# First products as 11 block products of sums of blocks in place of 12, over groups of 1024 tokens

## The chip, the cores and the metric

The kernel runs on one core of a Trainium2 chip. The metric is the device time of one execution in microseconds (us). TensorE multiplies, VectorE (DVE) and ScalarE (ACT) read its results out of PSUM banks, GpSimd (POOL) works on SBUF alone, SyncE (SP) issues the DMAs.

## The reference

Three layers over 3072 tokens (4 batches of 768) and a model width of 384:

```python
# 1: decayed linear attention, per batch and head (8 heads of 48)
state = f[t, :, None] * state + outer(k[t], v[t]);  y[t] = q[t] @ state
# 2: a mixture of 8 experts, all tokens through all experts
P = exp(logits - max); 8 rounds of normalizing P over rows, then columns
out = sum over e of P[:, e] * (relu(x @ w1[e]) @ w2[e])      # 384 -> 1024 -> 384
# 3: a bilinear layer
((x @ w_a) * (x @ w_b)) @ w_out                               # 384 -> 1536 -> 384
```

w_a, w_b and w_out come as float64; the rest is float32.

## The kernel before

Every product of float32 accuracy is made of three passes over split operands: a high part H (a ScalarE copy to fp32r) and a low part L (the rest); the passes are H·H, H·L and L·H.

**The attention stage** runs 24 steps of 128 tokens. Each step ends with six DMAs that bring y to x's layout (L593), a ScalarE copy into xH and a VectorE subtraction into xL (L599, L600). Expert 0 is computed beside it, in 12 blocks of 256 tokens (function expert0), as entries that fill TensorE's time; its low parts are made on GpSimd (L637), its results go to DRAM (y0, L653). xH and xL hold all 3072 tokens in SBUF. The order of the instructions of a stage is written out by class Plan: a list schedule in which each entry has a cost, a priority and the buffers that it reads and writes; GAP = 0.2 us is charged from one engine's end to another's start, and LATE = 4 us for a load. The engines then run that fixed order, each its own, and wait on semaphores.

**The main stage** (L734 on) has units of weights: 14 of 512 hidden columns (experts 1 to 7) and 6 of 256 (the last layer). For each unit it goes over 6 blocks of 512 tokens. front() makes the first products: for each tile of 128 hidden columns nine products of 512 tokens (gemm_f, L276: 3 k tiles x 3 passes) in one PSUM bank pF, then H on ScalarE and L on VectorE out of the bank. back() makes the second products (gemm_t, L288: 384 columns wide, bank pR) and VectorE adds them to acc, all of whose 24 token tiles are in SBUF. After the last expert unit x2_split transposes acc and splits it into xH and xL again. A unit's weights are loaded and split on ScalarE and GpSimd while the unit before is computed (add_piece, L247, L249); float64 weights go through seven VectorE operations (to_f32, L192 to L200), once, since each weight is loaded once. Instructions that the planner's loop emits in the main stage all carry L847.

Of the kernel before, what the change touches and what calls it, by code (L numbers as in the profile page):

```python
# [112 lines left out]
def kernel(  # L113
# [89 lines left out]
    def load_unit(parts, tag):  # L203
        """parts: dram access patterns, of [128, n, m] or in the order of ROWS; H and L of each."""
        views, pieces = [], []
        o = None
        for src in parts:
            if o is None or src is parts[-1]:
                tg = "i" if o is None else "o"
                o = 0  # L210
                wh = wpool.tile([128, WT[tg]], F32R, tag=f"{tag}{tg}h", name="wh")
                wl = wpool.tile([128, WT[tg]], F32R, tag=f"{tag}{tg}l", name="wl")
            n = src.shape[1 if len(src.shape) == 3 else 0]
            m = src.shape[-1] // (1 if src.dtype == F32 else 2)
            cut = m if src.dtype == F32 or m <= 256 else m // 2
            hv, lv = (t[:, o:o + n * m].rearrange("p (n m) -> p n m", n=n) for t in (wh, wl))
            for j in range(n):
                for c in range(0, m, cut):
                    pieces.append((src, hv, lv, cut, j, c))
            views.append((hv, lv))  # L220
            o += n * m
        return views, pieces

    def add_piece(plan, prio, key, src, hv, lv, cut, j, c):
        """The load of one part of a unit, its H, its L."""
        wide = src.dtype != F32
# [4 lines left out]

        def get():
            if len(src.shape) == 3:
                sj = src[:, j, 2 * c:2 * c + 2 * cut] if wide else src[:, j, c:c + cut]
                nc.sync.dma_start(out=raw, in_=sj if wide else sj.bitcast(I32))
                return
            for hd in range(2):
                nc.sync.dma_start(out=raw[64 * hd:64 * hd + 64], in_=src[j, hd, :, :, c:c + cut].bitcast(I32))

        plan.add(prio, "SP", .05 + cut * (.0013 if not wide else .0026), [], [f"raw{n}"], get, LATE)  # L240
        got, gk = f32(raw), f"raw{n}"
        if wide:
            for x, fn in enumerate(to_f32(raw, cut, *cvs)):
                plan.add(prio + 1 + x, "DVE", (.07 + cut / 960) * (1 if x % 2 or x == 4 else .65),
                         [gk], ["cv"], fn)
            got, gk = f32(cvs[0][:, :cut]), "cv"
        plan.add(prio + 9, "ACT", .1 + cut / 1200, [gk], [key], lambda: nc.scalar.activation(  # L247
            out=hj, in_=got, func=AF.Copy))
        plan.add(prio + 10, "POOL", .05 + cut * .0023, [gk, key], [key], lambda: nc.gpsimd.tensor_tensor(  # L249
            out=lj, in0=got, in1=f32(hj), op=ALU.subtract))  # L250
# [637 lines left out]
```

## Time and profile before

| | us |
|---|---|
| median of 3 runs (lowest, highest) | 2339.33 (2337.92, 2340.45) |
| span of the profiled execution | 2336.7 |
| TensorE products busy | 2285.6 (98%) |
| VectorE busy | 1132.5 (48%) |
| ScalarE busy | 645.1 (28%) |
| GpSimd busy | 254.8 (11%) |
| chain of waits: L276 into pF, L288 into pR | 42%, 36% |

The span runs from the first to the last instruction of one execution. Products are pipelined and overlap in the records, so what one costs is the distance between the starts of two. "Idle before" is the time in which an engine stood still ahead of an instruction, with what ended it. The granted clock is a share of 2.4 GHz.

### The profile page before, as it was taken

Reading aid. Unit: us, or ns where it says so; the run is one execution under the profiler, and the core shown is the slowest. Engines: PE = TensorE matmul, PEld = TensorE weight load, DVE = VectorE, ACT = ScalarE, POOL = GpSimd, SP = SyncE. Lnnn points to the kernel's source line nnn. Section 1 sums busy time; section 2 is a strip of 40 time slices with the busy share of each in tenths; the row PEclk is TensorE's granted clock in tenths of the full one; section 3 lists DMA queues with packets and bytes.
Section 4 is the critical chain, followed back from the end, with each engine's and each line's share of the span. In section 5 each row is a group of like instructions: output and inputs, shape, how many; then the busy total and the mean of one; then the engine's idle time right before and its main releaser. Section 6 shows DMA issues by size and latency. Waiting matters only on the chain.

```text
span 2336.7 us, 38096 instructions
## 1 busy us (share of the span) xinstructions
PE 2285.6 (98%) x15883; PEld 2072.8 (89%) x15883; DVE 1132.5 (48%) x2278; ACT 645.1 (28%) x1342; POOL 254.8 (11%) x291
## 2 busy tenths in 40 slices
PE   5999999999999999999999999999999999999999
PEld 4888888999999999999999999999999988888888
DVE  7888888443333333333333333333336564667643
ACT  3555555452121212112121111111212233222221
POOL 2221212230010101001010010100100010001000
PEclk8899999999999999999999999999999999999999
DMA  6444333140000000000000000000000010111001
GB/s 123 94 89 83 77 79 61 32 136 11 27 23 5 28 1 28 15 13 28 1 28 12 16 27 1 27 3 26 24 8 25 17 37 22 33 32 37 29 18 68
DMA packets 174316, 84.41 MB, mean 36 GB/s; under 512 B 133440, under 2 KB 163392, under 8 KB 174144
## 3 DMA queue, kind: packets, MB, share of 16 engines
q1 hardware_dynamic: 174144, 81.97, 14.1%
q8 instruction: 125, 2.05, 0.4%
q14 instruction: 47, 0.39, 0.1%
HBM read 67.78 MB, written 9.44 MB: 33 GB/s over the span
## 4 chain that ended last, share of the span: by engine, by line
PE 88%; DVE 7%; ACT 1%; SPq 1%; DMA 1%; issue 1%; POOL 0%; DVEq 0%; ACTq 0%; POOLq 0%
PE pF L276 42%; PE pR L288 36%; PE pM L288 3%; PE pM L276 3%; DVE fi L422 1%; DVE X L479 1%; DMA xf<-q 1%; PE pO L578 1%; SPq L593 1%; DVE X L528 1%; PE pA L454 1%; DMA raw<-in_moe_w_dram 1%; PE pA L442 0%; DVE fi L414 0%; DVE fi L416 0%
## 5 line engine op out<-in xcount | busy, mean ns | idle before, releaser
L276 PE MATMUL pF<-xH,wl 128*128 128x512 f32 x1440 | 562.7, 391 | 0.0
L276 PE MATMUL pF<-xL,wh 128*128 128x512 f32 x1440 | 562.3, 390 | 0.0
L276 PE MATMUL pF<-xH,wh 128*128 128x512 f32 x1440 | 561.7, 390 | 0.0
L288 PE MATMUL pR<-wh,gh 128*128 128x384 f32 x1632 | 547.7, 336 | 0.0
L288 PE MATMUL pR<-wh,gl 128*128 128x384 f32 x1632 | 546.9, 335 | 0.0
L288 PE MATMUL pR<-wl,gh 128*128 128x384 f32 x1632 | 546.0, 335 | 0.0
L847 ACT ACTIVATE gh<-pF 128x512 fp32r<-128x512 f32 x336 | 200.8, 598 | 978.7 <-PE pF L276 978.7
L847 DVE SCALAR_TENSOR_TENSOR gl<-pF,gh 128x512 fp32r<-128x512 f32 x336 | 232.1, 691 | 488.6 <-ACT gh L847 488.3
L847 DVE SCALAR_TENSOR_TENSOR acc<-pR,prob,acc 128x384 f32<-128x384 f32 x336 | 207.4, 618 | 410.7 <-PE pR L288 409.8
L276 PEld LDWEIGHTS pF<-xH,wl 128*128 128x128 f32 x1440 | 270.2, 188 | 56.7
L276 PEld LDWEIGHTS pF<-xL,wh 128*128 128x128 f32 x1440 | 270.2, 188 | 53.8
L276 PEld LDWEIGHTS pF<-xH,wh 128*128 128x128 f32 x1440 | 270.4, 188 | 53.2
L288 PEld LDWEIGHTS pR<-wh,gh 128*128 128x128 f32 x1632 | 306.4, 188 | 4.6
L288 PEld LDWEIGHTS pR<-wl,gh 128*128 128x128 f32 x1632 | 306.4, 188 | 4.7
L288 PEld LDWEIGHTS pR<-wh,gl 128*128 128x128 f32 x1632 | 306.2, 188 | 0.0
L249 POOL TENSOR_TENSOR wl<-raw,wh 128x384 fp32r<-128x384 f32 (+1 forms) x112 | 127.7, 1146 | 1152.0 <-ACT wh L247 1141.7
L637 POOL TENSOR_TENSOR hl<-hf,hh 128x256 fp32r<-128x256 f32 x96 | 80.0, 836 | 310.5 <-ACT hf L635 305.4
L847 DVE TENSOR_TENSOR a<-a,pF 128x512 f32<-128x512 f32 x72 | 49.5, 687 | 129.8 <-PE pF L276 126.6
L249 POOL TENSOR_TENSOR wl<-cva,wh 128x256 fp32r<-128x256 f32 (+1 forms) x60 | 42.1, 702 | 497.8 <-ACT wh L247 497.8
L276 PE MATMUL pM<-xH,wh 128*128 128x256 f32 x288 | 90.1, 313 | 0.1
L247 ACT ACTIVATE wh<-raw 128x384 fp32r<-128x384 f32 (+1 forms) x112 | 61.8, 565 | 98.6 <-DMA raw<-in_moe_w_dram 53.0
L276 PE MATMUL pM<-xL,wh 128*128 128x256 f32 x288 | 82.6, 287 | 0.7 <-DVE xL L600 0.7
(126 smaller groups left out, 2174.3 us busy)
## 6 DMA issues: line engine op xcount, KB each, us to landing
raw<-in_moe_w_dram SPq DMA_DIRECT2D x96, 128.0 KB, 2.6
raw<-in_moe_w_dram SPq DMA_DIRECT2D x64, 192.0 KB, 2.3
nat_f<-in_f_logit_dram SPq DMA_DIRECT2D x24, 192.0 KB, 3.3
nat_q<-in_q_dram SPq DMA_DIRECT2D x24, 192.0 KB, 3.4
nat_k<-in_k_dram SPq DMA_DIRECT2D x24, 192.0 KB, 3.7
vn<-in_v_dram SPq DMA_DIRECT2D x24, 192.0 KB, 2.7
Y<-in_v_dram SPq DMA_DIRECT2D x96, 48.0 KB, 2.8
xf<-q SPq DMA_DIRECT2D x144, 32.0 KB, 2.0
```

The lines of the kernel that those rows point to most:

```text
L247: plan.add(prio + 9, "ACT", .1 + cut / 1200, [gk], [key], lambda: nc.scalar.activation(out=hj, in_=got, func=AF.Copy))
L249: plan.add(prio + 10, "POOL", .05 + cut * .0023, [gk, key], [key], lambda: nc.gpsimd.tensor_tensor(out=lj, in0=got, in1=f32(hj), op=ALU.su ...
L276: nc.tensor.matmul(out=ps, lhsT=a[:, kk, fs], rhs=b[:, kk, ts], start=(i == 0), stop=(i == 3 * KD - 1),)
L288: nc.tensor.matmul(out=ps, lhsT=a[:, off:off + 128], rhs=b, start=(start and i == 0), stop=(stop and i == n - 1))
L422: op(DVE, .34, [], [f"fi0{z}", f"fi1{z}"], lambda a=a, c=c: nc.vector.tensor_tensor(out=fi[:, :, :, a], in0=fi[:, :, :, a], in1=fi[:, :, : ...
L454: nc.tensor.matmul(out=A1[o:o + 56, 0, g, :].rearrange("j (b e) -> j b e", e=8), lhsT=pct(k3)[r:r + D, g, 0:56], rhs=qv[r:r + D, g, :, 1, :])
L479: nc.vector.copy_predicated(X[r, hd].rearrange("j g (b two e) -> j g b two e", two=2, e=n)[:, :, :, 1, :], mbc(r, o, nb, n), A1[r, lv].rea ...
L528: op(DVE, .34, [f"q3{z}", f"g32{z}"], [f"Xq{z}"], lambda hd=hd, r=r: nc.vector.tensor_tensor(out=X[r, hd, :, 32:64], in0=pct(q3)[r, :, 32: ...
L578: nc.tensor.matmul(out=ps[64 * hd:64 * hd + D, p * 128 + 64 * c:p * 128 + 64 * c + 64], lhsT=Y[0:kk, hd, c, p, :], rhs=X[0:kk, hd, 2 * p + ...
L593: nc.sync.dma_start(out=xf[64 * hd:64 * hd + 64, kk, :], in_=yT[r:r + 16].rearrange("d (p t) -> d p t", p=NP))
L637: op(POOL, .64, [f"hh{ft}", kf], [f"hl{ft}"], lambda hh=hh, hl=hl, hf=hf: nc.gpsimd.tensor_tensor(out=hl, in0=hf, in1=f32(hh), op=ALU.subt ...
L847: fn()
```

## The change

Two halves of a pair of hidden tiles (256 columns) and two halves of 1024 tokens, over three k tiles, are a block product of 2 x 3 by 3 x 2 blocks: 12 block products in before. After, sums of blocks of the weights and of x are made first, and 11 block products of these, added up in an order of seven chains, give the same four results. One job is one pair of hidden tiles for 1024 tokens. In CHAINS a line names the bank, its products as (sum of weights, sum of x), and what the chain yields. A chain accumulates in one of three PSUM banks (A, B, C); b1, b2 and c1 are copied out by ScalarE to a buffer z while the bank goes on accumulating, and t1, t2 and t3 are added to a z by VectorE.

The main stage goes by six phases: expert phases of groups 0 and 1, last layer of group 0, experts of group 2, last layer of groups 1 and 2. x is stored to DRAM (xd) and the nine sums of a group are loaded, made and split at the start of its phase (for the first, in the attention stage on GpSimd). The weights are loaded and split anew for each group; each job's five sums of weight blocks and the low parts are made on GpSimd. The float64 weights are converted once, during the expert phases, and written to DRAM as float32. Expert 0 and the logits read x from two blocks of 256 tokens. acc holds the 8 token tiles of one group. back() works on four hidden tiles, in two parts, with the priority of the job three further on.

```diff
+X_SUMS = [(1,), (1, "add", 3), (3,), (2,), (0, "subtract", 3), (0, "add", 1), (4, "subtract", 1), (5,), (3, "add", 4)]
+W_RAW = [(0, 0), (2, 2), (1, 9)]
+W_SUMS = [(4, 10, 1), (5, 9, 4), (6, 0, 5), (7, 10, 9), (8, 3, 2)]
+CHAINS = [
+    ("B", [(4, 0)], "b1"),
+    ("A", [(1, 5), (3, 3)], "t1"),
+    ("B", [(5, 1)], "b2"),
+    ("C", [(9, 6), (2, 7)], "c1"),
+    ("B", [(6, 2)], "t2"),
+    ("C", [(7, 8), (8, 7)], "t3"),
+    ("B", [(2, 3), (0, 4)], "t0"),
+]
...
-    xH = big.tile([128, KD, NT], F32R, name="xH")
-    xL = big.tile([128, KD, NT], F32R, name="xL")
+    xsum = [[big.tile([128, TB], F32R, name=f"xs{x}{n}") for x in "hl"] for n in range(NX)]
+    xd = [spill.tile([KD, 128, NT], F32, name=f"x{n}d") for n in (1, 2)]
...
+    b_x = [[sba.tile([128, KD, EB], F32R, name=f"x{x}{n}") for x in "HL"] for n in range(2)]
...
+    def w1_prep(plan, prio, n):
...
+        for kk, slot in W_RAW:
+            plan.add(prio, SP, .38, [] if phases[ph][0] == "moe" else [f"wd{e}"], [f"sg{j}{kk}"], get, LATE)
+        sk = [f"sg{j}{kk}" for kk in range(KD)]
+        for o, a, b in W_SUMS:
+            plan.add(prio + 1, POOL, .4, sk, [f"sg{j}s"], partial(
+                nc.gpsimd.tensor_tensor, out=st[:, o], in0=st[:, a], in1=st[:, b], op=ALU.subtract))
+        for x in range(2):
+            s = slice(5 * x, 5 * x + 5)
+            key = f"w1{n % 3}{x}"
+            plan.add(prio + 2, ACT, .65, sk + [f"sg{j}s"], [key], partial(
+                nc.scalar.activation, out=wh[:, s], in_=st[:, s], func=AF.Copy))
+            plan.add(prio + 3, POOL, 1.6, sk + [f"sg{j}s", key], [key], partial(
+                nc.gpsimd.tensor_tensor, out=wl[:, s], in0=st[:, s], in1=f32(wh[:, s]), op=ALU.subtract))
...
+    def x_sum(plan, prio, i, src, tmp, eng):
...
+        if len(src) > 1:
+            (ka, a), (kb, b) = src
+            plan.add(prio, eng, ce, [ka, kb], [key], partial(
+                tt, out=t, in0=a, in1=b, op=getattr(ALU, X_SUMS[i][1])))
+        plan.add(prio, ACT, .6, [key], [f"xs{i}"], partial(nc.scalar.activation, out=xh, in_=t, func=AF.Copy))
+        plan.add(prio, eng, ce, [key], [f"xs{i}"], partial(tt, out=xl, in0=t, in1=f32(xh), op=ALU.subtract))
...
-    p_F = ring("pF", 4, [128, 512], psb)
-    p_R = ring("pR", 4, [128, 512], psb)
+    p_F = ring("pF", 5, [128, 512], psb)
+    p_R = ring("pR", 3, [128, 512], psb)
+    NH = 6
+    b_z = ring("z", 9, [128, TB], sbb)
+    acc = ring("acc", TPG, [128, DM], sbb)
...
+        for bank, prods, what in CHAINS:
...
+            def mm(prods=prods, ps=ps, new=new):
+                for slot, x in prods:
+                    xh, xl = xsum[x]
+                    for a, b in ((wh, xh), (wh, xl), (wl, xh)):
+                        nc.tensor.matmul(out=ps, lhsT=a[:, slot], rhs=b, start=(new and i == 0),
+                                         stop=(i == 3 * len(prods) - 1), skip_group_check=not new)
...
+            if what in ("b1", "b2", "c1"):
+                plan.add(prio, ACT, .6, [kp], [kz], partial(nc.scalar.activation, out=z, in_=ps, func=AF.Copy))
+                continue
+            ft, t = {"t0": (0, 0), "t1": (1, 0), "t2": (0, 1), "t3": (1, 1)}[what]
+            if what == "t0":
+                ky, y = kp, ps
+            else:
+                ky, y = got[{"t1": "b1", "t2": "c1", "t3": "b2"}[what]]
+                plan.add(prio, DVE, .7, [kp], [ky], partial(nc.vector.tensor_tensor, out=y, in0=ps, in1=y, op=ALU.add))
...
+    def back(n, hs, ws):
...
+        prio = 1000 * (n + 3)
...
+            for part in range(2):
+                hp = [hs[2 * part + i][j * 128 // TB] for i in range(2)]
+                wp = ws[2 * part:2 * part + 2]
+                plan.add(prio, PE, .173 * 6, [h[0] for h in hp] + [w[0] for w in wp], [kr], partial(
+                    gemm_t, ps, [h[1:] for h in hp], [w[1:] for w in wp], off, part == 0, part == 1))
...
+    def x2(prio, t, at, ka):
+        plan.add(prio, PE, .33, [ka], [kr], tr)
+        kz, z = take_z()
+        plan.add(prio, ACT, .45, [kr], [kz], partial(nc.scalar.activation, out=z[:, :DM], in_=ps[:, :DM], func=AF.Copy))
+        plan.add(prio, SP, .1, [kz], [f"xd1{t * 128 // TB}"], lambda: nc.sync.dma_start(
+            out=xd[1][:, :, t * 128:t * 128 + 128].rearrange("k p t -> p k t"),
+            in_=z[:, :DM].rearrange("p (k t) -> p k t", k=KD)), 3.0)
```

## Rows read from the trace of the kernel before

**Rows 1.** Page, part 1: busy us of each engine (share) x instructions.

```profile
PE 2285.6 (98%) x15883; PEld 2072.8 (89%) x15883; DVE 1132.5 (48%) x2278; ACT 645.1 (28%) x1342; POOL 254.8 (11%) x291
```

**Rows 2.** Chain that ended last: start us, us, what; mid main stage.

```profile
1119.74 8.20 PE pF L276 x36
...
1127.94 8.34 PE pR L288 x48
```

**Rows 3.** Groups by line and form: count, busy us, mean ns, idle before, releasers.

```profile
L276 PE MATMUL pF<-xH,wh 128*128 128x512 f32 x1440 | 561.7, 390 | 0.0
...
L288 PE MATMUL pR<-wh,gh 128*128 128x384 f32 x1632 | 547.7, 336 | 0.0
...
L847 DVE SCALAR_TENSOR_TENSOR gl<-pF,gh 128x512 fp32r<-128x512 f32 x336 | 232.1, 691 | 488.6 <-ACT gh L847 488.3
...
L847 DVE SCALAR_TENSOR_TENSOR acc<-pR,prob,acc 128x384 f32<-128x384 f32 x336 | 207.4, 618 | 410.7 <-PE pR L288 409.8 <-ACT acc L847 0.7
...
L249 POOL TENSOR_TENSOR wl<-raw,wh 128x384 fp32r<-128x384 f32 x64 | 65.8, 1030 | 151.9 <-ACT wh L247 141.6 <-DMA acc<-y 10.3
...
L249 POOL TENSOR_TENSOR wl<-raw,wh 128x512 fp32r<-128x512 f32 x48 | 61.9, 1300 | 1000.1 <-ACT wh L247 1000.1
...
L847 DVE TENSOR_TENSOR a<-a,pF 128x512 f32<-128x512 f32 x72 | 49.5, 687 | 129.8 <-PE pF L276 126.6 <-ACT wh L247 2.7
```

**Rows 4.** Busy us by window: PE, PEld, DVE, ACT, POOL, PEclk, DMA share, GB/s.

```profile
0.00:487.33 487.33, 439.77 (x6588) 401.99 (x6589) 378.64 (x870) 253.03 (x634) 106.10 (x136) 0.96 0.39 79
...
487.33:2336.70 1849.37, 1845.79 (x9297) 1670.81 (x9296) 753.88 (x1408) 392.05 (x708) 148.73 (x155) 1.00 0.08 25
```

**Rows 5.** Timeline of VectorE and GpSimd, float64 conversions: start us, us, instruction.

```profile
1900.26 0.28 DVE L199 TENSOR_SCALAR cvt<-raw 128x256 int32<-128x256 int32 x1
...
1900.58 0.43 DVE L200 SCALAR_TENSOR_TENSOR cva<-cvt,cva 128x256 f32<-128x256 int32 x1
...
1901.70 0.69 DVE L847 TENSOR_TENSOR gl<-a,gh 128x512 fp32r<-128x512 f32 x1 [0.69 <-ACT gh L847]
...
1902.04 0.94 POOL L249 TENSOR_TENSOR wl<-cva,wh 128x256 fp32r<-128x256 f32 x1 [5.45 <-ACT wh L247]
...
1902.30 0.83 DVE L192 TENSOR_SCALAR cvt<-raw 128x256 int32<-128x256 int32 x1
...
1924.39 0.60 POOL L249 TENSOR_TENSOR wl<-cva,wh 128x192 fp32r<-128x192 f32 x1 [4.47 <-ACT wh L247]
...
1924.43 0.69 DVE L847 TENSOR_TENSOR a<-a,pF 128x512 f32<-128x512 f32 x1 [0.52 <-PE pF L276]
```

**Rows 6.** Timeline, hand-overs TensorE to ScalarE, VectorE to TensorE.

```profile
1127.78 0.33 PE L288 MATMUL pR<-wh,gh 128*128 128x384 f32 x1
...
1127.98 0.60 ACT L847 ACTIVATE gh<-pF 128x512 fp32r<-128x512 f32 x1 [1.44 <-PE pF L276]
...
397.96 0.66 DVE L513 TENSOR_TENSOR k<-k,g 112x256 f32<-112x256 f32 x1
...
398.67 0.60 PE L518 MATMUL pO<-ident,k 112*128 112x112 f32 x4 [0.76 <-DVE k L513]
```

**Rows 7.** Timeline of ScalarE, attention stage.

```profile
390.92 0.38 ACT L632 ACTIVATE hh<-pM 128x256 fp32r<-128x256 f32 x1 [1.73 <-PE pM L276]
...
393.46 0.52 ACT L599 ACTIVATE xH<-xf 128x384 fp32r<-128x384 f32 x1
```

**Rows 8.** SP's queue: last stores of y0; line L238's issues (ns), its landing.

```profile
483.88 4.49 SPq L653 DMA_DIRECT2D y<-ys  x2
...
L238 SPq DMA_DIRECT2D raw<-in_moe_w_dram x96: 536/578/1812, 6.0 to 1675.1; - x96
...
DMA to landing us min/median/max: 2.3/2.6/5.3
```

**Rows 9.** Timeline of TensorE, then a window (as in rows 4).

```profile
403.98 1.15 PE L442 MATMUL pA<-bq,bk 48*64 48x64 f32 x32 [1.31 <-ACT bk L432]
...
406.00:407.00 1.00, 1.00 (x6) 0.80 (x4) 0.92 (x3) 0.68 (x2) 0.00 (x0) 0.50 0.00 0
```

More of the change, by code (lines that the diff above doesn't have):

```diff
@@ L201, in to_f32 @@
         ]
[L203 to L222, printed above, removed]
@@ L224, in add_piece, with take_raw @@
-    def add_piece(plan, prio, key, src, hv, lv, cut, j, c):
-        wide = src.dtype != F32
-        hj, lj = hv[:, j, c:c + cut], lv[:, j, c:c + cut]
+    def take_raw(m):
         n = count["raw"] % len(raws)
         count["raw"] += 1
-        raw = raws[n][:, :2 * cut if wide else cut]
-        def get():
[L233 to L250, printed above, removed]
@@ L270, in gemm_f, with add_piece @@
+    def add_piece(plan, prio, key, parts, hj, lj, reads=()):
+        m = hj.shape[-1]
+        rk, raw = take_raw(m)
+        def get():
+            for p0, n, src in parts:
+                nc.sync.dma_start(out=raw[p0:p0 + n], in_=src.bitcast(I32))
+        plan.add(prio, "SP", .05 + m * .0013, reads, [rk], get, LATE)
+        split_ops(plan, prio + 9, f32(raw), rk, hj, lj, key, m)
+    def gemm_f(ps, w, ft, x):
         wh, wl = w
+        xH, xL = x
         fs = slice(ft * 128, ft * 128 + 128)
-        ts = slice(t0, t0 + n)
@@ L646, in expert0 @@
                 fs = slice(part * n, part * n + n)
-                wk = [f"w{part // 2}o{x}" for x in range(KD, KD + FT)]
+                wk = [f"e0o{part // 2}{x}" for x in range(FT)]
                 op(PE, .98, hk + wk, [km], partial(
@@ L710 @@
     sinkhorn(plan, 1000 * NSTEP, 0, ROUNDS1, "T", p_T)
-    NUNIT = E * (DFF // FU)
-    NUNIT2 = DFF2 // FU2
-    units = [("moe", u) for u in range(NUNIT)] + [("out", u) for u in range(NUNIT2)]
-    views = {}
-    def load(plan, n, lo, hi, pieces):
-        for x in range(lo, hi):
-            key = f"w{n % 2}{'oi'[len(pieces) - x > n_out(n)]}{x}"
-            add_piece(plan, 1000 * NBLK * (n - 1) + 4000 * x / len(pieces) + 500, key, *pieces[x])
-    def n_out(n):
-        return FT if units[n][0] == "moe" else 2 * FT2
@@ L725 @@
-    NBLK = NT // 512
-    views[2], pieces2 = load_unit(moe_parts(2), "w0")
-    for x in range(KD):
-        add_piece(plan, 1000 * (NSTEP + 10) + x, f"w0i{x}", *pieces2[x])
+    phases = [("moe", 0), ("moe", 1), ("out", 0), ("moe", 2), ("out", 1), ("out", 2)]
+    jobs = []
+    for ph, (kind, g) in enumerate(phases):
+        for u in range((E - 1) * (DFF // FU) if kind == "moe" else DFF2 // FU):
+            for f in range(0, FT, 2):
+                if kind == "moe":
+                    jobs.append((ph, u, f, 1 + u // (DFF // FU), u % (DFF // FU) * FU + f * 128))
+                else:
+                    jobs.extend((ph, u, f, n, u * FU + f * 128) for n in range(2))
@@ new lines, with get @@
+    PW = 2 * 128
+    def w1_prep(plan, prio, n):
+        ph, _, _, e, c = jobs[n]
+        if phases[ph][0] == "moe":
+            parts = moe_rows(e, c, PW)
+        else:
+            parts = [[(0, 128, wd[e][kk * 128:kk * 128 + 128, c:c + PW])] for kk in range(KD)]
+        j = n % 2
+        st, (wh, wl) = stage[j], w1s[n % len(w1s)]
+        for kk, slot in W_RAW:
+            def get(kk=kk, slot=slot):
+                for p0, m, src in parts[kk]:
+                    nc.sync.dma_start(out=st[p0:p0 + m, slot:slot + 2, :].rearrange("p s f -> p (s f)"), in_=src)
+            plan.add(prio, SP, .38, [] if phases[ph][0] == "moe" else [f"wd{e}"], [f"sg{j}{kk}"], get, LATE)
[10 more added lines that the diff above has]
+                nc.gpsimd.tensor_tensor, out=wl[:, s], in0=st[:, s], in1=f32(wh[:, s]), op=ALU.subtract))
@@ L729 @@
+    prio = 1000 * 12
+    ab = [(f"xr{n}", b_xr[n]) for n in range(2)]
+    for blk, z, i in ((1, 0, 0), (3, 1, 2), (None, 0, 1), (0, 0, 4), (4, 0, 8), (1, 1, None), (4, 0, 6), (0, 0, 5),
+                      (2, 0, 3), (5, 1, 7)):
+        prio += 700
+        if blk is not None:
+            x_load(plan, prio - 400, 0, blk, *ab[z])
+        if i is not None:
+            x_sum(plan, prio, i, ab if len(X_OF[i]) > 1 else [], ab[z], POOL)
+    w1_prep(plan, 1000 * 12, 0)
     with tc.manual_schedule():
@@ new lines, with take_z, convert @@
+    xraw = {b: (f"xr{b}", sbb.tile([128, TB], F32, name=f"xr{b}")) for b in range(2 * KD)}
+    cva = ring("cva", 2, [128, 256], sbb, I32)
+    cvt = sbb.tile([128, 256], I32, name="cvt")
+    count["cv"] = 0
+    def take_z():
+        m = count["z"] % len(b_z)
+        count["z"] += 1
+        return f"z{m}", b_z[m]
+    def convert(prio, n, r0, c, m):
+        rk, raw = take_raw(2 * m)
+        x = count["cv"] % 2
+        count["cv"] += 1
+        src = (w_a, w_b, w_out)[n].bitcast(I32)[r0:r0 + 128, 2 * c:2 * c + 2 * m]
+        plan.add(prio, SP, .7, [], [rk], lambda: nc.sync.dma_start(out=raw, in_=src), LATE)
+        for i, fn in enumerate(to_f32(raw, m, cva[x], cvt)):
+            plan.add(prio + 1 + i, DVE, (.07 + m / 960) * (1 if i % 2 or i == 4 else .65),
+                     [rk], [f"cva{x}", "cvt"], fn)
+        plan.add(prio + 9, SP, .2, [f"cva{x}"], [f"wd{n}"], lambda: nc.sync.dma_start(
+            out=wd[n][r0:r0 + 128, c:c + m], in_=f32(cva[x][:, :m])), 3.0)
@@ new lines, in front @@
+    def front(n):
+        ph, u, f, ab, _ = jobs[n]
+        kind = phases[ph][0]
+        prio = 1000 * n
+        wh, wl = w1s[n % len(w1s)]
+        banks, got = {}, {}
+        hs = [[None, None], [None, None]]
+        if kind == "moe" or ab == 1:
+            for ft in range(2):
+                for t in range(2):
+                    m = count["h"] // 4 * 2 % NH + ft
+                    hs[ft][t] = (f"g{t}{m}", *b_h[t][m])
+            count["h"] += 4
+        for bank, prods, what in CHAINS:
+            prio += 10
+            new = bank not in banks
+            if new:
+                banks[bank] = take("F", p_F)
+            kp, ps = banks[bank]
+            def mm(prods=prods, ps=ps, new=new):
+                i = 0
+                for slot, x in prods:
[3 more added lines that the diff above has]
+                                         stop=(i == 3 * len(prods) - 1), skip_group_check=not new)
+                        i += 1
+            plan.add(prio, PE, .227 * 3 * len(prods), [f"xs{x}" for _, x in prods] +
+                     sorted({f"w1{n % 3}{s // 5}" for s, _ in prods}), [kp], mm)
+            if what in ("b1", "b2", "c1"):
+                kz, z = take_z()
+                got[what] = kz, z
+                plan.add(prio, ACT, .6, [kp], [kz], partial(nc.scalar.activation, out=z, in_=ps, func=AF.Copy))
[3 more added lines that the diff above has]
+                ky, y = kp, ps
+            else:
+                ky, y = got[{"t1": "b1", "t2": "c1", "t3": "b2"}[what]]
+                plan.add(prio, DVE, .7, [kp], [ky], partial(
+                    nc.vector.tensor_tensor, out=y, in0=ps, in1=y, op=ALU.add))
+            if kind == "out" and ab == 0:
+                if what == "t0":
+                    ky, y = take_z()
+                    plan.add(prio, ACT, .6, [kp], [ky], partial(
+                        nc.scalar.activation, out=y, in_=ps, func=AF.Copy))
+                a_of[what] = ky, y
+                continue
+            kh, hh, hl = hs[ft][t]
@@ L783, in front @@
                 nc.vector.tensor_tensor, out=hl, in0=a, in1=f32(hh), op=ALU.subtract))
         return hs
-    def back(n, b, hs):
-        kind, u = units[n]
-        later = n == len(units) - 1 and b == NBLK - 2
-        prio = 1000 * (NBLK * n + b + later) + 100
-        w = ftiles(views[n][-1])
-        hk = [f"g{x}{m}" for m, _, _ in hs for x in "hl"]
-        hp = [h[1:] for h in hs]
-        for j in range(TPB):
-            t = b * TPB + j
+    def back(n, hs, ws):
+        ph, u, _, e, _ = jobs[n]
+        kind, g = phases[ph]
+        last = n + 1 == len(jobs) or jobs[n + 1][0] != ph
+        prio = 1000 * (n + 3)
+        for j in range(TPG):
+            t = g * TPG + j
@@ L838 @@
[L838 to L844 removed]
+                nc.tensor.transpose(ps[:, kk * 128:kk * 128 + 128], at[:, kk * 128:kk * 128 + 128], ident)
+        plan.add(prio, PE, .33, [ka], [kr], tr)
+        kz, z = take_z()
```

224 lines of the change are left out of this document (119 added, 105 removed).

## The prediction

> **What bounds the kernel now.** I read the busy times first [rows 1]: TensorE's products are busy 2285.6 us of a span of 2336.7 us. Busy time counts overlapped products, so the chain of waits comes next [rows 2]. From the middle of the kernel to its end it is TensorE alone: 36 products of 512 columns in 8.20 us, then 48 of 384 columns in 8.34 us, each piece beginning where the one before ended (1119.74 + 8.20 = 1127.94). So one 512-column product costs 8.20/36 = 0.2278 us and one 384-column product 8.345/48 = 0.1738 us, far below their busy means of 390 and 336 ns [rows 3]. The windows [rows 4] cut the span at 487.33 us, the first product of the main stage: before it TensorE is busy 439.8 of 487.3 us; after it 1845.8 of 1849.4 us, at a granted clock of 1.00 (2.4 GHz). In the main stage VectorE is busy 753.9 us (41%), ScalarE 392 (21%), GpSimd 149 (8%). TensorE is the bound there with no hole, and fewer products pay in full as long as no hole opens.
>
> The span is taken as 2336.7 us; the median of the runs, 2339.33, lies 2.6 above it, and I put the differences on the median.
>
> **Products removed.** The main stage has 3 x 1440 = 4320 products of 512 columns [rows 3]. After: 84 jobs of the expert layer (3 groups x 7 experts x 1024/256) and 36 of the last layer (3 x 1536/256 x 2), each 11 blocks x 3 passes = 33 products, 3960 in all. 360 x 0.2278 = 82.0 us go, all on the path. The second products stay: 42 x 8 x 12 + 9 x 8 x 12 = 4896, as 3 x 1632 now.
>
> **Work added beside them.** In time of TensorE an expert job is 33 x 0.2278 + 48 x 0.1738 = 15.9 us. VectorE per job: three additions of a PSUM bank to a copy in SBUF at 0.687 (the row of a<-a,pF has these operands), four low parts at 0.691, four accumulations at 0.618 [rows 3]: 7.3 us. In jobs 3 to 56 comes one float64 conversion, four operations with two inputs at 0.43 and three with one at 0.28 [rows 5]: 2.5, so 9.8 of 15.9. ScalarE: seven at 0.60, two splits of 640 and two of 384 columns: about 7. GpSimd from 1030 ns for 384 and 1300 ns for 512 columns [rows 3], 2.1 ns a column: 0.49 for a sum of 128, 1.57 for 640; 5 x 0.49 + 2 x 1.57 + 2 x 1.03 = 7.7 us. A last-layer pair needs 14 x 0.69 + 2.2 = 12 us of VectorE and 13 of GpSimd in 66 x 0.2278 + 48 x 0.1738 = 23.4. No engine becomes the bound by its sum.
>
> **New waits inside a job.** One bank now takes a chain, is read, and takes the next. TensorE's end to ScalarE's start is 0.20 (1127.78 to 1127.98), VectorE's end to TensorE's start 0.05 (398.62 to 398.67) [rows 6]. So a ScalarE copy returns a bank in 0.20 + 0.60 + 0.05 = 0.85 us, a VectorE addition in 0.94. Between b1 and b2, and between t2 and t0, lie six products, 1.37 us: covered by 0.52 and 0.43. Between c1 and t3 lie only three, 0.68: short by 0.17. The planner sees this (it charges 0.2 for each hand-over, and costs near these rows), and from the third job it has second products of the pair before, 1.04 us each, to put there. What it does not know is how two engines disturb each other.
>
> At 1902.04 a GpSimd difference of 256 columns began under a VectorE operation with both inputs in SBUF and took 0.94; VectorE's next, a one-input operation from SBUF to SBUF, took 0.83 where the same form took 0.28, and ended as GpSimd did. At 1924.43 VectorE's a<-a,pF, with one input in PSUM, ran beside a GpSimd operation in its usual 0.69 [rows 5]. So operations wholly in SBUF exclude each other, and one with a PSUM input passes. Before, GpSimd is busy 8% of the main stage and most low parts read PSUM. After, GpSimd is at half, three of four low parts read z in SBUF, and conversions move into the expert phases. If each of 3 + 7 such operations lost 0.83 - 0.28 = 0.55 us, VectorE would need 9.8 + 5.5 = 15.3 of 15.9 us: still under, but late against its plan, and the slack before t0 is 0.43 us. I charge 0.1 us of TensorE per job, 12 us; bounds 0 and 0.35 us (half of 0.55, and some), 0 to 42.
>
> The Trainium skill (SBUF — State Buffer, SBUF: two separate sides) calls the pair of ports that VectorE and GpSimd share "an **exclusive lock**, not a bandwidth split", held for a whole instruction, also against VectorE operations with two SBUF inputs. The trace agrees (0.83 for 0.28, and 0.69 unchanged with PSUM). It speaks against this change, and its strict form is a rival below.
>
> **Start of the main stage.** Now the first product follows expert 0's last at once. After, only job 0's weights are ready. Job 1's loads stand on SP's queue behind the last stores of expert 0, which go out until 488.4; six DMAs at 0.58 us, 2.6 to land [rows 8], five sums 2.4, ScalarE 0.7, first low half 1.6: about 499.3. Job 0 ends at 487.3 + 7.5 = 494.8. 4.5 us of stall, about 1 more before job 2: 6 us, bounds 2 and 12.
>
> **Changes of phase.** Five times the nine sums of x are made anew. Under them TensorE has the last second products, 16 x 1.04 = 16.7 us. Where expert phases end (three times) the nine z buffers are the catch: eight go to the transposed x, and the sums and first copies of the next job take them again only when the stores have landed. From tile 6's last product: 0.2 + 0.62 + transposes and copy 1.1 + store 0.33 + landing 2.6 + copy 0.85 = 5.7 us, over which lie tile 7 (2.1) and chains of the next two jobs (about 2); those jobs then run without fill. A hole also costs clock: after 1.31 us of idle time ahead of the small products at 403.98 TensorE's granted clock reads 0.50 (1.2 GHz) at 406 [rows 9]; I estimate 1 to 2 us a time. I take 5 us each, 15, and 2 each for the two others, 4; bounds 4 and 60.
>
> **Attention stage.** Removed: three weight splits (about 3 x 1.3 of GpSimd). Added: 24 stores and 6 loads of x on SP, 14 GpSimd operations at 1.30, one weight preparation, 24 us of GpSimd in a stage where VectorE is busy 379 of 487 us [rows 4], mostly in SBUF. x now lives in two blocks: step 20's x waits until expert 0 has read block 8, whose first result is at 390.92 while step 20's came at 393.46 [rows 7]; block 8 needs some 20 us. But x is the end of a step, xf has two buffers, and TensorE has expert 0 meanwhile. 4 us, bounds -4 and 25. The end costs 1 us: the last h takes about 2.3 us, and 3 banks of first halves (3.1 us) lie over it.
>
> Sum: -82 + 12 + 6 + 15 + 4 + 4 + 1 = -40; 2339.3 - 40 = 2299 us.
>
> **Rivals.**
> 1. All is covered. The planner's hand-over of 0.2 exceeds the 0.05 measured, so its order has slack. Start 3, phases 5, else 0: 2339.3 - 82 + 8 = 2265. For it: zero holes now. Against: the start and z chains are counted out of rows.
> 2. The borders decide: 10 at the start, 12 at each of five changes, 8 in attention: 2339.3 - 82 + 78 = 2335. For it: no fill in two jobs, and the clock. Against: parts of those chains overlap.
> 3. The lock decides, slower. Place: VectorE's queue between t2's addition and chain t0. If in each job the addition stands behind one operation blocked by a 1.57 us GpSimd difference, it is late by up to 1.57 + 0.69, less 0.43 of slack, 1.83; half of it, 0.9, x 120 = 108, with 30 for the rest: 2339.3 - 82 + 138 = 2395. It decides from (82 - 30)/120 = 0.43 us per job. For it: the 0.83 row, GpSimd at half. Against: TensorE's stall gives VectorE time to catch up, and VectorE is free 38% or more.
>
> **How the numbers follow.** Forecast 0.55 (its own range 2278 to 2320), rival 1 0.20, rival 2 0.13, rival 3 0.12. No change is within 0.2%, 4.7 us, which is what this kernel's runs can tell (2337.92 to 2340.45). Slower: rival 3 nearly whole: 0.11. Same: the middle of rival 2: 0.05. Faster: 0.84. The range 2266 to 2336 leaves out some 0.06 below and 0.14 above.
>
> **What would show it.** 3960 products of 512 columns at 0.2278 us in unbroken pieces; holes of TensorE of a few us after the first job and at five borders, with the clock lower behind them; inside jobs, holes released by VectorE ahead of the t0 chains or by ScalarE ahead of t3, some 12 us in total and most in jobs 3 to 56; VectorE's operations from SBUF longer than 0.69, those from PSUM not. It is wrong if the attention stage ends over 25 us later, if TensorE's idle time inside jobs is over 0.43 us each, or if a chain's change of bank costs time of itself.

## The result, and the profile after

The changed kernel takes 2359.9 us (median of four runs, 2359.2 to 2365.35) beside 2339.86 of the kernel before on the same chip: ratio 1.0094, 95% interval 1.008 to 1.0108. It is 20 us slower where 40 us less was forecast, and outside the range 2266 to 2336. Its profiled execution spans 2357.6 us, 20.9 over the 2336.7 of before.

The products did go. The groups by line of the kernel after (count, busy us, mean ns, idle before, releasers):

```profile
L846 PE MATMUL pF<-xsh,w1h 128*128 128x512 f32 x1320 | 525.2, 398 | 47.2 <-DVE gl L979 28.2 <-DVE z L979 12.7 <-ACT z L979 5.8
...
L979 DVE TENSOR_TENSOR z<-pF,z 128x512 f32<-128x512 f32 x378 | 258.8, 686 | 253.8 <-PE pF L846 203.5 <-ACT z L979 45.5 <-ACT w1h L979 2.8
L979 DVE SCALAR_TENSOR_TENSOR gl<-z,gh 128x512 fp32r<-128x512 f32 x252 | 214.1, 862 | 80.7 <-ACT gh L979 78.2 <-POOL w2l L235 1.3
...
L221 DVE TENSOR_TENSOR cva<-cva,cvt 128x256 f32<-128x256 f32 x36 | 32.1, 892 | 0.2
L222 DVE TENSOR_SCALAR cvt<-raw 128x256 int32<-128x256 int32 x36 | 31.5, 874 | 0.5
...
L979 POOL TENSOR_TENSOR w1l<-stage,w1h 128x640 fp32r<-128x640 f32 x238 | 404.6, 1713 | 259.8 <-ACT w1h L979 242.8 <-PE pF L846 11.3 <-DMA stage<-in_moe_w_dram 5.1
```

Three groups of 1320 first products stand for three of 1440 [rows 3], but idle time that was 0.0 ahead of each is 47.2 us ahead of one, and VectorE released 41 of it. VectorE's addition from PSUM (z<-pF) kept the 0.69 of before. The low part with both inputs in SBUF (gl<-z) takes 0.86 on average, and two of a conversion's seven operations, which took 0.42 and 0.29 on average in the kernel before, now take 0.89 and 0.87. The two in the kernel before:

```profile
L198 DVE TENSOR_TENSOR cva<-cva,cvt 128x256 f32<-128x256 f32 x36 | 15.2, 421 | 0.8
...
L199 DVE TENSOR_SCALAR cvt<-raw 128x256 int32<-128x256 int32 x36 | 10.5, 291 | 0.9
```

Windows of the kernel after (length, then busy us of PE, PEld, DVE, ACT, POOL, PEclk, DMA share, GB/s): the part ahead of the main stage; most of jobs 4 to 27; one hole in them and the stretch behind it; jobs without conversions.

```profile
0.00:495.65 495.65, 440.75 (x6587) 402.14 (x6588) 391.32 (x870) 258.11 (x642) 127.36 (x154) 0.98 0.43 90
559.90:955.00 395.10, 374.68 (x1860) 337.87 (x1859) 272.61 (x445) 147.26 (x258) 177.51 (x212) 0.98 0.25 73
598.82:600.83 2.01, 0.17 (x2) 0.01 (x1) 2.01 (x5) 0.00 (x0) 0.27 (x1) 1.00 0.00 0
601.00:604.00 3.00, 3.00 (x8) 2.36 (x9) 1.71 (x5) 0.57 (x2) 0.00 (x0) 0.54 0.56 166
1620.00:2000.00 380.00, 380.00 (x1936) 347.53 (x1935) 185.86 (x264) 153.44 (x267) 188.27 (x220) 1.00 0.19 55
```

In the second row TensorE is idle 20.4 of 395 us with VectorE busy 69% of it; in the last, where no weights are converted, it is idle for nothing although GpSimd works half the time. So the expert jobs of the new form do run without a hole when VectorE has only its own work. There the chain of waits has whole pieces again, at the price per product of before (10.24/45 = 0.2276, 14.58/84 = 0.1736):

```profile
1669.69 14.58 PE pR L275 x84
1684.28 10.24 PE pF L846 x45
```

**One hole, read through three engines.** Timeline of TensorE after (start us, us, instruction, idle time before with its releaser):

```profile
598.65 0.34 PE L275 MATMUL pR<-w2h,gl 128*128 128x384 f32 x1
600.83 0.50 PE L846 MATMUL pF<-xsh,w1h 128*128 128x512 f32 x1 [1.84 <-DVE gl L979]
...
604.47 0.43 PE L275 MATMUL pR<-w2h,gh 128*128 128x384 f32 x1
```

VectorE in the same stretch:

```profile
595.53 1.53 DVE L221 TENSOR_TENSOR cva<-cva,cvt 128x256 f32<-128x256 f32 x1
596.98 0.68 DVE L979 SCALAR_TENSOR_TENSOR gl<-z,gh 128x512 fp32r<-128x512 f32 x1
597.59 1.65 DVE L222 TENSOR_SCALAR cvt<-raw 128x256 int32<-128x256 int32 x1
599.15 0.68 DVE L979 SCALAR_TENSOR_TENSOR gl<-z,gh 128x512 fp32r<-128x512 f32 x1
599.76 0.41 DVE L223 SCALAR_TENSOR_TENSOR cva<-cvt,cva 128x256 f32<-128x256 int32 x1
600.09 0.68 DVE L979 SCALAR_TENSOR_TENSOR gl<-pF,gh 128x512 fp32r<-128x512 f32 x1
```

and GpSimd, with ScalarE's copy out of t0's bank in the last line:

```profile
595.21 1.57 POOL L979 TENSOR_TENSOR w1l<-stage,w1h 128x640 fp32r<-128x640 f32 x1 [1.26 <-ACT w1h L979]
597.47 1.61 POOL L979 TENSOR_TENSOR w1l<-stage,w1h 128x640 fp32r<-128x640 f32 x1 [0.70 <-ACT w1h L979]
...
596.18 0.58 ACT L979 ACTIVATE gh<-pF 128x512 fp32r<-128x512 f32 x1
```

GpSimd's second difference ran from 597.47 to 599.08. The conversion step at 597.59, 0.28 us by itself, ended at 599.24; the step at 595.53 had been held in the same way by the first difference (1.53 for 0.42). Behind them in VectorE's order stood the low part of t0. Its inputs were ready at 596.76, when ScalarE ended, but it began at 600.09. It empties t0's bank, and with a ring of five banks that bank is the C bank of the next job: the c1 chain, the fourth of that job, takes it, and TensorE stood 1.84 us. Nine products then took 3.64 us (600.83 to 604.47), not 9 x 0.2278 = 2.05, at a granted clock of 0.54: the hole cost 1.84 and the clock behind it 1.6. Not every hole pays for the clock. The one that ends at 636.28 was as long, and the clock behind it reads 1.00; of the ten holes over 1.5 us in jobs 4 to 27, four were followed by a lower one.

```profile
636.28:639.28 3.00, 3.00 (x14) 2.61 (x15) 2.43 (x6) 1.13 (x2) 0.08 (x1) 1.00 0.52 157
```

In the expert jobs the low part of t0 is the releaser in 19 waits of TensorE (28.2 us). In the last layer the same bank is emptied by VectorE's product of two results (z<-pF,z), and 8.0 of the 12.7 us put down to z<-pF,z are four waits for it. No conversion runs there; two operations of VectorE's own work are held instead, 2.04 us each for 0.69, beside two 640-column differences of GpSimd (VectorE, GpSimd, TensorE):

```profile
2137.57 2.04 DVE L979 TENSOR_TENSOR z<-z,z 128x512 f32<-128x512 f32 x1
2139.53 2.04 DVE L979 TENSOR_TENSOR gl<-z,gh 128x512 fp32r<-128x512 f32 x1
2141.49 0.68 DVE L979 TENSOR_TENSOR z<-pF,z 128x512 f32<-128x512 f32 x1
...
2137.49 3.53 POOL L979 TENSOR_TENSOR w1l<-stage,w1h 128x640 fp32r<-128x640 f32 x2 [4.08 <-ACT w1h L979]
...
2142.22 0.50 PE L846 MATMUL pF<-xsh,w1h 128*128 128x512 f32 x1 [2.01 <-DVE z L979]
```

At the place named in the prediction, t2's addition late ahead of t0, there are two waits, 2.1 us.

**Where the time went.** As lost time of the main stage I count what the starts of successive products lie apart beyond 0.2278 and 0.1738 us. By groups of jobs, in the kernel after and in six experiments (us, each from one profiled execution and rounded):

| stretch | after | e1 | e2 | e4 | e5 | e7 | e8 |
|---|---|---|---|---|---|---|---|
| main stage begins at | 495.7 | 501.4 | 498.1 | 497.7 | 498.0 | 493.9 | 494.7 |
| jobs 0-3 (start) | 10.5 | 11.0 | 9.5 | 11.4 | 9.3 | 13.9 | 15.6 |
| 4-27, 32-35 (256-column conversions) | 33.8 | 2.7 | 1.1 | 8.2 | 7.7 | 7.7 | 1.1 |
| 36-53 (192-column) | 3.2 | 0.7 | 0.6 | 1.7 | 4.9 | 1.8 | 0.7 |
| 70-93 (none) | 1.0 | 0.9 | 1.7 | 1.9 | 1.8 | 0.9 | 0.9 |
| last-layer jobs | 16.3 | 16.3 | 0.1 | 2.7 | 2.9 | 7.2 | 0.6 |
| five changes of phase | 30.9 | 28.4 | 13.8 | 17.6 | 25.3 | 7.7 | 4.4 |
| sum | 95.7 | 60.1 | 26.7 | 43.5 | 51.8 | 39.1 | 23.2 |

The whole span follows: main stage 8.3 later (495.65 for 487.33), 95.7 lost there for 1.35 before, 82.0 removed, 0.3 at the end: 8.3 + 95.7 - 1.35 - 82.0 + 0.3 = 20.9.

The 8.3 is the least sure of these terms. e1, e2 and e3 (below) leave the attention stage as it is in the kernel after, and their main stages begin at 501.4, 498.1 and 498.6, so a difference of up to 6 us at this place can't be told from single executions.

### The profile page after: what moved, and what is told of

It reads as the page before. It is cut to its first block, busy times and chain, and to the rows that moved or that the text cites. A ratio compares the mean times of both kernels' runs of the same rounds, so it can differ in the third digit from the quotient of the medians.

```text
span 2357.6 us, 41276 instructions
## 1 busy us (share of the span) xinstructions
PE 2240.2 (95%) x15523; PEld 2011.2 (85%) x15523; DVE 1529.4 (65%) x2612; ACT 1028.2 (44%) x1988; POOL 1033.8 (44%) x1191
## 4 chain that ended last, share of the span: by engine, by line
PE 71%; DVE 20%; issue 3%; ACT 2%; SPq 2%; DMA 1%; POOL 0%; DVEq 0%; ACTq 0%; POOLq 0%
PE pR L275 34%; PE pF L846 30%; DVE z L979 3%; DVE gl L979 3%; PE pM L263 2%; PE pM L275 2%; DVE fi L413 2%; DVE X L470 1%; DVE cvt L222 1%; DVE cva L221 1%; DVE X L519 1%; DVE fi L407 1%; PE pO L569 1%; ACT z L979 1%; DVE fi L405 1%
## 5 line engine op out<-in xcount | busy, mean ns | idle before, releaser
L846 PE MATMUL pF<-xsh,w1h 128*128 128x512 f32 x1320 | 525.2, 398 | 47.2 <-DVE gl L979 28.2
L275 PE MATMUL pR<-w2h,gh 128*128 128x384 f32 x1632 | 549.3, 337 | 8.0 <-DVE acc L979 3.5
L275 PE MATMUL pR<-w2h,gl 128*128 128x384 f32 x1632 | 548.0, 336 | 0.1
L275 PE MATMUL pR<-w2l,gh 128*128 128x384 f32 x1632 | 546.9, 335 | 0.0
L846 PE MATMUL pF<-xsh,w1l 128*128 128x512 f32 x1320 | 521.5, 395 | 0.3 <-POOL w1l L979 0.2
L846 PE MATMUL pF<-xsl,w1h 128*128 128x512 f32 x1320 | 521.1, 395 | 0.0
L979 POOL TENSOR_TENSOR w1l<-stage,w1h 128x640 fp32r<-128x640 f32 x238 | 404.6, 1713 | 259.8 <-ACT w1h L979 242.8
L275 PEld LDWEIGHTS pR<-w2h,gh 128*128 128x128 f32 x1632 | 307.2, 188 | 17.3 <-DVE acc L979 4.7
L275 PEld LDWEIGHTS pR<-w2l,gh 128*128 128x128 f32 x1632 | 307.0, 188 | 6.6
L275 PEld LDWEIGHTS pR<-w2h,gl 128*128 128x128 f32 x1632 | 306.7, 188 | 0.7 <-DVE gl L979 0.7
```

The lines of the kernel that those rows point to most:

```text
L275: nc.tensor.matmul(out=ps, lhsT=a[:, off:off + 128], rhs=b, start=(start and i == 0), stop=(stop and i == n - 1))
L846: nc.tensor.matmul(out=ps, lhsT=a[:, slot], rhs=b, start=(new and i == 0), stop=(i == 3 * len(prods) - 1), skip_group_check=not new)
L979: fn()
```

## The experiments

Each starts from the changed kernel unless it says otherwise; each ratio is to the kernel before, run again beside it (2339.7 or 2338.9 us). Every run is planned anew, so the order of instructions can differ too. My theory: GpSimd's long operations hold VectorE's SBUF operations up, and TensorE waits for VectorE. Its rivals: VectorE simply has too much work; the ring of five banks is too short; the order was planned with wrong durations.

**e1: VectorE's conversion work taken away, but for the first of seven operations**

```
-        for i, fn in enumerate(to_f32(raw, m, cva[x], cvt)):
+        for i, fn in enumerate(to_f32(raw, m, cvt, cva[x])[:1]):
```

> The kernel after, but of a conversion's seven VectorE operations only the first is kept (the float32 weights of the last layer are then not the weights; every DMA stays). After takes 2359.9 us; jobs 4 to 35, which hold the 256-column conversions, lose 34 us of TensorE beyond its products. Theory lock (GpSimd's operations block VectorE's from SBUF to SBUF, VectorE hands t0's bank back late, TensorE waits for it in the next job's c1 chain): these 34 us go nearly whole, 2322 to 2332 us. Theory work (the conversions cost VectorE more than their planned time, GpSimd or not): the same. Theory banks (the order of the chains over five banks stalls by itself): under 10 us, 2350 to 2360.

Measured: 2325.96 us, ratio 0.9943 to before (0.9929 to 0.9958). The conversion jobs lose 2.7 us for 33.8; the last-layer jobs, which have no conversions, lose 16.3 as they did. GpSimd's operations are no shorter (w1l 1770 ns for 1713), and the low part held up by them takes even longer, 962 ns for 862:

```profile
L979 DVE SCALAR_TENSOR_TENSOR gl<-z,gh 128x512 fp32r<-128x512 f32 x252 | 239.3, 962 | 88.3 <-ACT gh L979 84.9
```

So in the conversion jobs holds alone did not stop TensorE. That they stop it when VectorE's queue is dense is one reading; but in these jobs the order of the instructions differs from the changed kernel's too, and e1, as expected, does not separate a hold from mere work.

**e2: GpSimd's long operations taken away**

```
-            plan.add(prio + 3, POOL, 1.6, sk + [f"sg{j}s", key], [key], partial(
-                nc.gpsimd.tensor_tensor, out=wl[:, s], in0=st[:, s], in1=f32(wh[:, s]), op=ALU.subtract))
+            if n < 3:
+                plan.add(prio + 3, POOL, 1.6, sk + [f"sg{j}s", key], [key], partial(
+                    nc.gpsimd.tensor_tensor, out=wl[:, s], in0=st[:, s], in1=f32(wh[:, s]), op=ALU.subtract))
```

> The kernel after, but GpSimd makes the low parts of the summed first weights only for jobs 0 to 2 (later jobs multiply by old low parts); its 640-column operations of 1.7 us go, the conversions stay whole on VectorE. Theory lock: VectorE's operations fall back to 0.42 and 0.28, the 34 us of the conversion jobs go for the most part, and some of the 15 us inside the last-layer phases: 2310 to 2330 us. Theory work: VectorE's own work is the same, so under 10 us goes: 2350 to 2360. Theory banks: the same as work.

Measured: 2293.55 us, ratio 0.9807 (0.9793 to 0.9822), better than I expected. All conversions are there, yet the conversion jobs lose 1.1 us and the last-layer jobs 0.1; over half of the loss at the changes of phase goes as well (13.8 for 30.9). Its window of the same stretch, columns as above:

```profile
559.90:955.00 395.10, 394.16 (x2019) 360.77 (x2018) 260.51 (x480) 158.20 (x277) 107.20 (x170) 1.00 0.28 81
```

VectorE does 480 operations in 260.5 us where the changed kernel did 445 in 272.6, and TensorE is idle 0.9. TensorE's order in jobs 4 to 27 and 32 to 53 is product for product that of the changed kernel: a new order of TensorE is not what took the holes away. VectorE's amount of work by itself is thus not the cause. e1 and e2 each remove nearly the whole loss of the conversion jobs (31.1 and 32.7 of 33.8): the holes there need the long holds (e2) and, as far as e1 shows it with its new order, the conversions in VectorE's queue as well. In the last layer they came without conversions.

**e3: six banks for first products**

```
-    p_F = ring("pF", 5, [128, 512], psb)
-    p_R = ring("pR", 3, [128, 512], psb)
+    p_F = ring("pF", 6, [128, 512], psb)
+    p_R = ring("pR", 2, [128, 512], psb)
```

> The kernel after with six PSUM banks for the chains and two for the second products (five and three before), so that no job's C bank is the bank whose t0 the job before has just ended. Theory banks, and lock if the place is this bank: TensorE's waits for VectorE's gl, 28 of its 60 us of listed waits, go, with the slow clock behind them: 2315 to 2335 us. Theory work, if VectorE is late in sum: the wait is found at another bank, within 8 us of 2360. Two banks for second products can cost: then up to 2370.

Measured: 2457.53 us, ratio 1.0511 (1.0489 to 1.0532): a miss, and it does not answer its question. The waits of the weight loads (us in all, times, longest) name the two banks left for second products:

```profile
PEld pR L275 <- DVE acc L979: 80.0, 30, 4.4
```

The waits for t0's low part are gone from the top of the list, but the bank came from where it cost more. Whether a sixth bank by itself would have hidden the holes stays open, since this run had to take it from the second products.

**e4: the same work of GpSimd in shorter operations**

```
-            plan.add(prio + 3, POOL, 1.6, ... out=wl[:, s], in0=st[:, s], in1=f32(wh[:, s]) ...
+            for y in range(5 * x, 5 * x + 5):
+                plan.add(prio + 3, POOL, .45, ... out=wl[:, y], in0=st[:, y], in1=f32(wh[:, y]) ...
```

> The kernel after, the same work, but each 640-column low part on GpSimd is made by five operations of 128 columns (about 0.5 us each in place of 1.7). Theory lock, by the length that one operation holds: the worst VectorE operation falls from 2.06 to under 1.2 us, half of the stalls in conversion jobs go: 2335 to 2350 us. Theory lock, by GpSimd's total time alone: GpSimd works longer (five starts for one), 2358 to 2375. Theory work: no change, 2355 to 2363.

Measured: 2312.52 us, ratio 0.9885 (0.987 to 0.99), 22 us better than the best that I expected. GpSimd's groups by form:

```profile
L980 POOL TENSOR_TENSOR w1l<-stage,w1h 128x128 fp32r<-128x128 f32 x1190 | 601.9, 537 | 154.8 <-ACT w1h L980 137.0 <-PE pF L847 8.3 <-DMA stage<-in_moe_w_dram 6.7
```

GpSimd works 197 us longer for these parts (601.9 for 404.6) and the kernel is 47 us faster. TensorE's order in jobs 4 to 27 and 32 to 53 is again that of the changed kernel. VectorE at the same place in the order:

```profile
596.61 0.48 DVE L221 TENSOR_TENSOR cva<-cva,cvt 128x256 f32<-128x256 f32 x1
597.01 0.95 DVE L980 SCALAR_TENSOR_TENSOR gl<-z,gh 128x512 fp32r<-128x512 f32 x1
597.88 0.55 DVE L222 TENSOR_SCALAR cvt<-raw 128x256 int32<-128x256 int32 x1
598.35 0.94 DVE L980 SCALAR_TENSOR_TENSOR gl<-z,gh 128x512 fp32r<-128x512 f32 x1
```

and GpSimd beside it, ten operations in one row:

```profile
596.93 5.61 POOL L980 TENSOR_TENSOR w1l<-stage,w1h 128x128 fp32r<-128x128 f32 x10
```

Under unbroken work of GpSimd each operation of VectorE now loses about 0.27 us (0.95 for 0.68, 0.55 for 0.28) and not 1.37 (1.65 for 0.28). What counts is the length of one hold, not GpSimd's share. That agrees with the exclusive lock, held for a whole instruction, which the prediction cites from the Trainium skill (SBUF — State Buffer, SBUF: two separate sides).

**e5: the same instructions, planned with measured durations**

```
+    COST = (.32, .57, .36, .50, .90, .87, .66)
-            plan.add(prio + 1 + i, DVE, (.07 + m / 960) * (1 if i % 2 or i == 4 else .65), ...
+            plan.add(prio + 1 + i, DVE, COST[i] * (1 if m == 256 else .8), ...
-                plan.add(prio, DVE, .7, [ky], [kh], ...
+                plan.add(prio, DVE, .69 if what == "t0" else 0.86, [ky], [kh], ...
```

and so for the other costs that had means in the trace (sums 0.52, first copies 0.74, low parts 1.71, accumulation 0.62).

> The kernel after with one thing changed: the planner's costs are the means that the trace of after shows (a low part from z 0.86 and 0.99 us in place of 0.70, a product of two z 1.14 for 0.70, a 256-column conversion 4.2 us in all for 2.0, GpSimd 1.71 and 0.52 for 1.6 and 0.4). The instructions are the same, their order is not. Theory length of hold (one 1.7 us operation makes a single VectorE operation up to 1.4 us late, which no mean foresees): a third of the 34 us in jobs 4 to 35 goes, 2340 to 2355 us. Theory order (TensorE waits because its order was made for a VectorE that is never late in the mean): nearly all goes, 2315 to 2330.

Measured: 2318.81 us, ratio 0.9914 (0.9899 to 0.9928). No instruction differs from the changed kernel's, only their order. The holds are all there, a little worse:

```profile
L981 DVE SCALAR_TENSOR_TENSOR gl<-z,gh 128x512 fp32r<-128x512 f32 x252 | 246.0, 988 | 77.4 <-ACT gh L981 76.2
```

and VectorE is busy 1545 us for 1529, yet 41 us come back: 26 in the conversion jobs, 13 in the last-layer jobs. Around the place of the hole TensorE now has three groups of six second products per pair of jobs where it had two: an order made for a slow VectorE puts work of TensorE over the hold. The measured time lies where the theory of order had it (2315 to 2330). So the plan is nearly as much a cause as the length of the holds. It does not help the change of phase in jobs 94 to 101 (about 11 us there for about 7).

**e6: a third block of x in the attention stage**

```
-    b_x = [[sba.tile([128, KD, EB], F32R, name=f"x{x}{n}") for x in "HL"] for n in range(2)]
+    b_x = [[sba.tile([128, KD, EB], F32R, name=f"x{x}{n}") for x in "HL"] for n in range(3)]
-    b_ys = ring("ys", 2, [128, DM])
+    b_ys = ring("ys", 1, [128, DM])
...
```

> The kernel after with three blocks of x for expert 0 in the attention stage in place of two, and one buffer in place of two for expert 0's results on their way to DRAM. The attention stage of after ends 8.3 us later than before (495.65 against 487.33), 6.6 of it as idle time of TensorE between 150 and 250 us. Theory ring (a step's x waits until expert 0 has read an older block): the main stage starts at 486 to 490 us, in all 2351 to 2355. Theory lock in the attention stage (GpSimd's sums of 512 columns hold VectorE up): it starts at 494 to 498, in all 2357 to 2363.

Measured: 2362.62 us, ratio 1.0103 (1.0086 to 1.012); the main stage begins at 501.3, not at the 486 to 490 expected if the ring of blocks were the cause. That speaks against the two blocks of x, for which the prediction reserved up to 25 us, but it does not rule them out: what the lost ys buffer costs is not separated, and the unchanged attention stage of e1 ended as late (501.4).

**e7: e4, with GpSimd's sums of x in four pieces, and 14 z buffers**

```
+        cuts = [slice(c, c + 128) for c in range(0, TB, 128)] if eng == POOL else [slice(0, TB)]
-            plan.add(prio, eng, ce, [ka, kb], [key], ... out=t, in0=a, in1=b ...
+            for s in cuts:
+                plan.add(prio, eng, ce, [ka, kb], [key], ... out=t[:, s], in0=a[:, s], in1=b[:, s] ...
...
-    b_z = ring("z", 9, [128, TB], sbb)
+    b_z = ring("z", 14, [128, TB], sbb)
```

> The kernel of the run with low parts in five pieces (2312.5 us), and the attention stage's sums of x on GpSimd in four pieces of 128 columns each, and 14 buffers z in place of nine. Main stage start there 497.65. Theory lock in the attention stage: it starts at 488 to 493; theory ring: 496 to 500. Changes of phase: in that run the jobs 28 to 31, 54 to 61 and 94 to 101 lose 6.9, 4.9 and 4.8 us; if the nine z buffers are the cause, as the prediction's chain has it, 10 of these 16.6 go; if not, under 3. In all 2295 to 2303 if both hold, 2305 to 2313 if neither does.

Measured: 2300.36 us, ratio 0.9836 (0.9821 to 0.9851). The first edit acts in the attention stage alone, the second in the main stage alone. The main stage begins at 493.9 for 497.7 in e4, but starts vary by more than that. TensorE's idle time between 150 and 250 us, where the 1.3-us sums of x run on GpSimd, says it more clearly: 7.4 us in e7 and 7.5 in e8, 9.8 to 12.1 in the seven kernels with whole sums (11.1 after, 12.1 in e4), 4.7 before. Short sums thus give back a part. And the three ends of expert phases lose 7.5 us for 16.6 in e4: the nine z buffers were 9 us. Not all of that is gained, because the last-layer jobs lose 7.2 us for 2.7 in e4; two waits for VectorE's additions to acc are 2.4 us each there for 0.8, and the run does not show why they grew.

**e8: all holds short, and the plan told of them.** e7, with the low parts of the second weights in pieces of 128 columns too, and costs as e4's trace had them.

```
+        for c in range(0, m, 128):
+            plan.add(prio + 1, "POOL", .52, [gk, key], [key], partial(
+                nc.gpsimd.tensor_tensor, out=lj[:, c:c + 128], in0=got[:, c:c + 128], in1=f32(hj[:, c:c + 128]),
...
+    COST = (.36, .60, .34, .44, .62, .43, .58)
...
```

> The kernel of the run before this one, with the low parts of the second weights in three pieces of 128 columns as well, and the planner's costs set to what the run with five pieces shows (low part from z 0.82, conversion 3.4 us in all, and so on). Theory length of hold: no operation of GpSimd in the main stage is longer than 0.6 us; the 7 us left in jobs 4 to 27 go, and some of the start: 2285 to 2297 us. Theory total time of GpSimd: it works 80 us longer, 2305 to 2320.

Measured: 2284.27 us, ratio 0.9768 (0.9753 to 0.9782): 55 us faster than the kernel before, 76 faster than the change as it was, and a little better than expected; what the shorter pieces and the new costs give is not separated here. Windows of e8, columns as above:

```profile
0.00:494.66 494.66, 445.29 (x6588) 405.90 (x6588) 381.08 (x870) 257.73 (x642) 159.45 (x238) 0.97 0.43 90
559.90:955.00 395.10, 395.10 (x2018) 361.66 (x2017) 270.41 (x480) 159.27 (x281) 273.98 (x537) 1.00 0.27 81
```

The 395 us that had 20.4 us of holes have none, with GpSimd busy 274 of 395 us and VectorE 270: the share of neither engine is the limit. Of the 23.2 us still lost 15.6 lie in jobs 0 to 3. There TensorE waits for ScalarE's z 2.7 us, for a bank that VectorE's normalizing of P (sk_c) holds 2.3 and for low parts of GpSimd 2.2, with the clock behind each; I made no run for it.

## Why the prediction was wrong

- **Products removed, -82.0: right**, in count and price.
- **In-job stalls: the step that failed.** "I charge 0.1 us of TensorE per job, 12 us; bounds 0 and 0.35 us" against 54.3 us (33.8 + 3.2 + 1.0 + 16.3), 0.45 a job. Of the 61 us between the forecast and the result, 42 lie in this term. The mechanism was named and its row was at hand (0.83 for 0.28 [rows 5]), but the size came from it wrongly, and the 0.1 was chosen, not worked out. That row was a 256-column difference; the new ones have 640 columns, and I had worked out 1.57 us for them a paragraph earlier and still priced each meeting at 0.55. e4 and e5 show the two things missed: the length of one hold, and an order written for durations without holds, which has no place for them. The price in TensorE's clock (1.6 us behind the hole shown, nothing behind others) was counted at the borders alone.
- **The place.** I looked for the wait between t2 and t0 with 0.43 us of slack. Two waits, 2.1 us, lie there; 36.2 us (28.2 and 8.0) are for t0's bank at the next job's c1 chain, which the prediction did not follow round the ring.
- **Changes of phase: 19 forecast, 31 measured**, inside the bounds. The z chain was 9 of them (e7), the long holds most of the rest (e2, e8). **Start: 6, measured 10.5**, and not for the reason given: no wait of TensorE there is for job 1's weights; the longest, 3.36 us from 504.33, is for a bank that VectorE's normalizing of P holds (sk_c). **Attention: 4, measured 8.3** and 11 to 14 in e1 to e3, inside the bounds: in part the long holds (e7, e8); no run shows the ring of x to be a part (e6), and the rest stays open. **End: 1, measured 0.3.**
- **The rivals.** Rival 3, the lock, is what happened, smaller than its 2395 and at another place: it was to decide from 0.43 us a job with 30 us for the rest, and the kernel stood at 0.45 with 49 (8.3 + 10.5 + 30.9 + 0.3, less 1.35). Its chance of 0.12 looks too low in hindsight. Its argument against, that VectorE is free 38% and catches up, holds over a phase but not within the few us of a bank's return. Rival 2's borders came to 50 of its 78 us. Rival 1's 2265, with nothing but borders left, is 19 us below e8.
- **No engine the bound by its sum: right**; jobs 70 to 93 lose 1.0 us in about 380 as they were changed.

## What to carry to other kernels

Before work moves to GpSimd, take its longest single operation, not its busy share, and put that whole length ahead of any VectorE operation with all operands in SBUF; cut it into pieces as short as VectorE's slack, even where the pieces cost GpSimd half as much again. Follow each bank round its ring to the next chain that takes it: the wait shows there, not where the late result is used. When an order is planned from costs, give it the durations measured beside the other engines, since the same instructions in a better order were worth 41 us here.

## What the hardware showed that was not expected

- The hold struck VectorE's operations wholly in SBUF, one-input int32 ones too (1.65 for 0.28); the longest gl<-z took 2.06 us, its shortest 0.67. With one input in PSUM none of the 378 operations z<-pF,z took over 0.69.
- GpSimd's fp32 difference beside a busy VectorE: 1713 ns on average for 640 columns, 537 for 128 (e4). From these two I estimate 2.3 ns a column and about 0.24 us fixed, which gives 1.13 us for 384 columns where 1.03 was measured; five pieces cost 2.69 for 1.71.
- A single hole of 1.84 us was followed by a granted clock of 0.54 over 3 us, near the lower level of 1.2 GHz, and nine products took 1.6 us more; behind another of 1.84 us the clock stayed at 1.00.
